# A fused sigmoid attention and SiLU MLP on one core: second matmul started per batch, loads gated in order of use, four score steps around each values group

## The chip, the cores and the metric

The kernel runs on one core of one Trainium2 chip. The metric is the device time of one execution in microseconds (us). Medians of repeated runs are quoted. A verdict of faster or slower needs 2%. "Span" is the profiled time from first to last instruction, some 2 us less than the run's time.

## The reference, cut to what matters

Attention with a sigmoid in place of softmax feeds a two-matrix MLP with SiLU. There are 8 batches, 12 heads, 448 positions and head size 64; the MLP goes from 768 to 2048 and back to 768.

```python
scores = scale * np.matmul(q, k.transpose(0, 1, 3, 2)) - np.log(S)
attn = 1.0 / (1.0 + np.exp(-scores))
x = matmul(attn, v)             # heads merged: (8*448, 768)
h = x @ w_in                    # 768 -> 2048
g = h * (1.0 / (1.0 + np.exp(-h)))
out = g @ w_out                 # 2048 -> 768
```

## The kernel before

The 12 heads of a batch are handled as 3 quads of 4. A quad takes 7 **score steps**: four 64x64 matmuls into one PSUM tile `psc` of two banks, then one sigmoid on ScalarE that writes fp16 attention weights. After 7 steps a **values group** (28 matmuls, `pav`) multiplies them with v. The MLP is a stream of **first-matmul units** (`ph`, 12 matmuls, then a sigmoid on ScalarE and a product on VectorE) and **second-matmul units** (`po`, 32 matmuls, half the columns of 128 output rows). The kernel fixes the order of the instructions on each engine (`manual_schedule`), and the timelines show the work of TensorE (PE) in the Python order below.

```python
ps_sc = tile_pool(name="ps_sc", bufs=2, PSUM)     # two score buffers (4 banks)
ps_1  = tile_pool(name="ps_1",  bufs=4, PSUM)     # everything else   (4 banks)

def scores(b, i, r):
    psc = ps_sc.tile([P, 2, 512], F32, ...)
    for t in range(2):
        for j in range(2):
            nc.tensor.matmul(psc[half(j), t, :S], kT[half(t), r, half(j)], qT[half(t), :, half(j)], ...)
    nc.scalar.activation(attn[b, i][:, :, r, :], psc[:, :, :S], AF.Sigmoid, bias=bias_s, scale=QKSCALE)

# batch 0: attention alone, with dummy matmuls ("idle") between the steps
for i in range(NQ):
    for r in range(R):
        scores(0, i, r)
        ...
        elif r == 3:
            ...
            load_w_in(i)           # quarters 0, 1, 2 of w_in
        if r == 0:
            stage(1, i)            # q and k of batch 1
load_v(1)                          # v of batch 1, behind three quarters of w_in
load_w_in(3)
values(0, NQ - 1)

# batches 1 to 7: two score steps, a values group if one is due, then some GEMM
for n in range(0, len(steps) + VISIT, VISIT):              # VISIT = 2
    for b, i, r in steps[n : n + VISIT]:
        scores(b, i, r)
    if done:
        values(*done.pop())
    ...                                                    # loads, casts, transposes
    if n < len(steps):
        gemm(T_FIRST if steps[n][0] == 1 else T_VISIT)
gemm(1e9)                                                  # the rest of the stream
```

The stream works on pairs of batches: first matmul of batches 0 and 1, then second matmul of both. While batch 1's attention runs, only batch 0's first matmul (16 units) is there to fill PE. v, w_in and w_out are loaded by the GpSimd queue (they are cast on the way), q, k and the transposes by the SyncE queue. One round of the loop, up to its GEMM, is called a **visit** here.

Of the kernel before, what the change touches and what calls it, by code (L numbers as in the profile page):

```python
# [10 lines left out]
F16 = mybir.dt.float16  # L11
F32 = mybir.dt.float32
# [5 lines left out]
def kernel(  # L18
# [13 lines left out]
    nc = tc.nc  # L32

    B, H, S, D = q.shape
    NT, DMODEL = out.shape
    DFF = moe_w_in.shape[1]
    P = 128
# [13 lines left out]
    ps_1 = ctx.enter_context(tc.tile_pool(name="ps_1", bufs=4, space=bass.MemoryType.PSUM))  # L51

    ET = mybir.EngineType
    ctx.enter_context(tc.manual_schedule(engines={ET.PE, ET.Pool, ET.DVE, ET.Activation}))

    qkT = {}
    v16s = {}
# [14 lines left out]

    w_in_sb = cpool.tile([P, NCC, DFF], F16, tag="w_in_sb", name="w_in_sb")
    w_out_sb = cpool.tile([P, NFC, DMODEL], F16, tag="w_out_sb", name="w_out_sb")

    def half(i):
        return slice(i * D, (i + 1) * D)

    def matmul2(ps, lhsT, rhs, start, stop):

        for i in range(2):
            nc.tensor.matmul(ps[half(i)], lhsT[:, half(i)], rhs, start=start, stop=stop)  # L82
# [12 lines left out]
    def load_w_in(step: int):  # L95

        w = DFF // 4
        f = slice(step * w, (step + 1) * w)
        for t in range(2):
            nc.gpsimd.dma_start(  # L100
                w_in_sb[half(t), :, f],
                moe_w_in[t * NCC * D : (t + 1) * NCC * D, f].rearrange("(c d) f -> d c f", d=D),
            )

    def load_w_out(s: int):
        nc.gpsimd.dma_start(
            w_out_sb[:, 4 * s : 4 * s + 4, :],
            moe_w_out[4 * s * P : (4 * s + 4) * P, :].rearrange("(fc p) e -> p fc e", p=P),
        )

    def stage(b: int, i: int, split: bool = False):
        tiles = [
            p2.tile([P, 2, R * D], F32, tag=f"st{nm}", name=f"st{nm}_{b}_{i}", bufs=3)
            for nm in "qk"
        ]
        staged[b, i] = tiles
        for st, src in zip(tiles, (q, k)):
            for t in range(0, 2, 1 if split else 2):
                tn = 1 if split else 2
                pairs_of = src[b].rearrange("(t i j) (p r) d -> i (j p) t (r d)", t=2, j=2, r=R)  # L120
                nc.sync.dma_start(st[:, t : t + tn], pairs_of[i][:, t : t + tn])

    def load_v(b: int, i0: int = 0, i1: int = NQ):
        if i0 == 0:
# [25 lines left out]
    def transpose_dma(b: int, i: int, nm: str):  # L150
        xt = new_T(b, i, nm)
        nc.sync.dma_start_transpose(xt, x16s.pop((nm, b, i)).rearrange("p r t d -> p (r t d)"))
# [14 lines left out]
    def scores(b: int, i: int, r: int):  # L167
        qT, kT = qkT["q", b, i], qkT["k", b, i]
        if r == 0:
            attn[b, i] = p2.tile([P, 2, R, S], F16, tag="attnT", name=f"attnT_{b}_{i}")  # L170
        psc = ps_sc.tile([P, 2, 512], F32, tag="pssc", name=f"psc_{b}_{i}_{r}")
        for t in range(2):
            for j in range(2):
                nc.tensor.matmul(  # L174
                    psc[half(j), t, :S], kT[half(t), r, half(j)], qT[half(t), :, half(j)],
                    start=True, stop=True,
                )
        nc.scalar.activation(  # L178
            attn[b, i][:, :, r, :], psc[:, :, :S], AF.Sigmoid, bias=bias_s, scale=QKSCALE
        )  # L180

# [31 lines left out]
    out_rows = out.rearrange("(b p r) e -> b r p e", b=B, r=R)  # L213

    def h_unit(b, fc):
        m = b // 2
        if m not in gTs:
            gTs[m] = cpool.tile([P, NFC, 2 * S], F16, tag="gTr", name=f"gTr_{m}")
        ph = ps_1.tile([P, 512], F32, tag="ps1", name=f"ph_{b}_{fc}")
        for cc in range(NCC):  # L220
            matmul2(
                ph[:, :S],
                w_in_sb[:, cc, fc * P : (fc + 1) * P],
                xTs[b][:, cc, :],
                cc == 0,
                cc == NCC - 1,
            )
        tsig = p2.tile([P, S], F16, tag="tsig", name=f"tsig_{b}_{fc}", bufs=3)
        nc.scalar.activation(tsig, ph[:, :S], AF.Sigmoid, bias=0.0, scale=ISX)  # L229
        nc.vector.tensor_mul(  # L230
            gTs[m][:, fc, (b % 2) * S : (b % 2) * S + S], ph[:, :S], tsig
        )

    T_H = NCC * 0.187
    T_O = NFC * 0.160 / 2

    def gemm_stream():
        for m in range(B // 2):
            for b in (2 * m, 2 * m + 1):
                while b not in x_done:  # L240
                    yield None
                for fc in range(NFC):
                    h_unit(b, fc)
                    yield T_H
            for g in range(2 * S // P):
                osb = p2.tile([P, DMODEL], F32, tag="osb", name=f"osb_{m}_{g}", bufs=3)
                for nh in range(2):
                    po = ps_1.tile([P, 512], F32, tag="ps1", name=f"po_{m}_{g}_{nh}")
                    for fc in range(NFC):
                        matmul2(  # L250
                            po[:, :NO2],
                            gTs[m][:, fc, g * P : (g + 1) * P],
                            w_out_sb[:, fc, nh * NO2 : (nh + 1) * NO2],
                            fc == 0,
                            fc == NFC - 1,
                        )
                        if fc == NFC // 2 - 1:
                            yield T_O
                    nc.vector.tensor_scalar_mul(
                        osb[:, nh * NO2 : (nh + 1) * NO2], po[:, :NO2], ISX  # L260
                    )
                    yield T_O
                for s in range(2):
                    bl, r = divmod(2 * g + s, R)
                    nc.sync.dma_start(out_rows[2 * m + bl, r], osb[half(s)])

    stream = gemm_stream()
    clock = [0.0, 0.0]

    def gemm(us: float):  # L270
        clock[1] += us
        while clock[0] < clock[1]:
            t = next(stream, None)
            if t is None:
                return
            clock[0] += t
# [16 lines left out]
    for i in range(NQ):  # L293
        nxt = (0, i + 1) if i + 1 < NQ else (1, 0)
        for r in range(R):
            scores(0, i, r)
            if r == 0 and i > 0:
                values(0, i - 1, 0, 4)
            elif r == 1 and i > 0:
                values(0, i - 1, 4, R)  # L300
            elif r == 2:
                transpose_pe(*nxt, "q")
            elif r == 3:
                transpose_pe(*nxt, "k")
                b2, i2 = (nxt[0], nxt[1] + 1) if nxt[1] + 1 < NQ else (1, 0)
                cast(b2, i2, "q", nc.vector)
                cast(b2, i2, "k", nc.gpsimd)
                load_w_in(i)
            else:
                idle(3, f"{i}_{r}")  # L310
            if r == 0:
                stage(1, i)
    load_v(1)
    load_w_in(3)
    values(0, NQ - 1)


    steps = [(b, i, r) for b in range(1, B) for i in range(NQ) for r in range(R)]
    VISIT = 2
    T_FIRST = NFC * T_H / (NQ * R) * VISIT  # L320
    T_VISIT = (NFC * T_H + S / P * NFC * 2 * 0.160) / (NQ * R) * VISIT
    done = []
    for n in range(0, len(steps) + VISIT, VISIT):
        for b, i, r in steps[n : n + VISIT]:
            scores(b, i, r)
        if done:
            values(*done.pop())
        for b, i, r in steps[n : n + VISIT]:
            if r == R - 1:
                done.append((b, i))  # L330
            if r == 0:
                if (b, i) == (1, 2):
                    load_w_out(0)
                    load_w_out(1)
                elif (b, i) == (2, 0):
                    load_w_out(2)
                    load_w_out(3)
                if b + 1 < B:
                    stage(b + 1, i)
                    if i == 0:  # L340
                        load_v(b + 1)
            if r == 3:
                if b == 1 and i + 1 < NQ:
                    for nm in "qk":
                        transpose_pe(1, i + 1, nm)
                    if i + 2 < NQ:
                        cast(1, i + 2, "q", nc.vector)
                        cast(1, i + 2, "k", nc.gpsimd)
                if b + 1 < B:
                    for nm in "qk":  # L350
                        cast(b + 1, i, nm, nc.gpsimd)
                        transpose_dma(b + 1, i, nm)
        if n < len(steps):
            gemm(T_FIRST if steps[n][0] == 1 else T_VISIT)
    gemm(1e9)


# [28 lines left out]
```

## Time and profile before

| | |
|---|---|
| median of runs | 416.78 us (416.7 to 417.35) |
| profiled span | 414.6 us |
| PE busy | 395.6 us, 95% |
| first scores on PE | 8.2 us |
| last matmul ends | 409.7 us |

The first lines are from the page of the kernel before: busy us, share of the span and instructions of PE, then PE's busy tenths, the granted clock and the traffic in 40 slices of 10.4 us.

```profile
PE 395.6 (95%) x5020; PEld 237.8 (57%) x5020; DVE 152.2 (37%) x254; ACT 222.6 (54%) x298; POOL 55.0 (13%) x71
...
PE   7899398999999999999999999999999999999995
...
PEclk9999799999999999999999999999999999999999
...
GB/s 264 306 275 263 185 272 135 190 225 263 185 71 266 298 26 2 125 276 69 77 59 216 294 92 2 98 105 2 77 40 77 40 40 2 2 2 40 78 77 76
```

PE is the limit almost everywhere. One dip stands out: the fifth slice (41 to 52 us) has PE at 3 tenths. Traffic is at 263 to 306 GB/s in the slices before it.

The next lines list what PE waited for in the kernel before: us in total, number of times, longest.

```profile
PE pav_1_0_944 L195 <- DMA v_1_677<-in_v_dram: 6.9, 1, 6.9
...
PE psc_0_1_1291 L174 <- ACT attnT_2_1107 L178: 1.0, 1, 1.0
...
PE psc_0_2_1297 L174 <- ACT attnT_0_1276 L178: 0.5, 1, 0.5
...
PE psc_2_1_1114 L174 <- ACT attnT_1_889 L178: 0.4, 1, 0.4
PE psc_2_5_1232 L174 <- ACT attnT_2_1107 L178: 0.4, 1, 0.4
PE psc_1_0_890 L174 <- ACT attnT_0_713 L178: 0.4, 1, 0.4
```

The largest wait is for v of batch 1; the five others shown are scores that wait for ScalarE to free a score buffer, all in batch 1 or at the start of batch 2. (Left out between them are short waits of the first 25 us, among them 1.2 us for v of batch 0.) The timeline of PE around the largest wait (start us, duration us, engine, line, operation, tiles):

```profile
41.15 0.36 PE L174 MATMUL psc_1_2_938<-qT_1_777,kT_1_794 64*64 64x448 f16 x4
48.44 0.58 PE L195 MATMUL pav_1_0_944<-attnT_0_713,v_1_677 64*64 64x448 f16 x2 [6.93 <-DMA v_1_677<-in_v_dram]
...
48.81 0.58 PE L195 MATMUL pav_1_0_944<-attnT_0_713,v_1_677 64*64 64x448 f16 x2
...
51.20 2.11 PE L82 MATMUL ph_7_977<-xT_401,w_in_sb 128*64 128x448 f16 x12
```

A values pair normally starts every 0.187 us; behind the wait it starts every 0.37 us, and the 12 matmuls of `ph_7` take 2.1 us where 1.3 is usual. The clock has been halved and needs until 53 us to return.

A visit with a values group in the steady part of the kernel before, PE and ScalarE (ACT), lines in between left out:

```profile
148.78 0.38 PE L174 MATMUL psc_2_0_2554<-qT_2_1920,kT_2_1924 64*64 64x448 f16 x4
...
148.99 0.36 PE L174 MATMUL psc_2_1_2560<-qT_2_1920,kT_2_1924 64*64 64x448 f16 x4
...
149.33 1.00 ACT L178 ACTIVATE attnT_2_2553<-psc_2_0_2554,bias_s 128x896 f16<-128x896 f32 x1
...
150.22 1.01 ACT L178 ACTIVATE attnT_2_2553<-psc_2_1_2560,bias_s 128x896 f16<-128x896 f32 x1
150.31 0.35 PE L195 MATMUL pav_3_1_2566<-attnT_1_2277,v_3_1289 64*64 64x448 f16 x2
...
150.60 1.32 PE L82 MATMUL ph_5_2602<-xT_1570,w_in_sb 128*64 128x448 f16 x12
```

Durations of matmuls overlap, so the cost of a unit is read from start to start: a score step 0.19 us, the values group 1.31, a first-matmul unit 1.14, a second-matmul unit 2.60. From one `ph` to the first score costs 0.09 us more than between two `ph`, from the last 64-row matmul back to `ph` 0.10 more (150.31 to 150.60, where 0.19 is usual), and the first units after each change another 0.055: 0.245 us for each **return** from 128-row to 64-row matmuls and back. In this visit PE never waits, but one should note when ScalarE lets go of the second score buffer: 150.22 + 1.01 = 151.23.

### The profile page before, as it was taken

The numbers are of one execution on the slowest core, as the hardware profiler recorded it, in microseconds if no ns is written. First come the engines' busy times: TensorE is split into PE (matmuls) and PEld (weight loads), VectorE is DVE, ScalarE is ACT, GpSimd is POOL, SyncE is SP. The second block draws the span as 40 slices with busy tenths as digits, with TensorE's granted clock in tenths as the row PEclk, the third lists the DMA queues.
The fourth block names the chain that finished last, engine by engine and source line by source line (L and its number), as shares of the span: only waits on it lengthen the run. The fifth ranks groups of instructions, "written<-read, shape, count | busy, mean of one in ns | idle before, by whom it ended". The sixth has DMA issues, their size and how long they took to land.

```text
span 414.6 us, 11185 instructions
## 1 busy us (share of the span) xinstructions
PE 395.6 (95%) x5020; PEld 237.8 (57%) x5020; DVE 152.2 (37%) x254; ACT 222.6 (54%) x298; POOL 55.0 (13%) x71
## 2 busy tenths in 40 slices
PE   7899398999999999999999999999999999999995
PEld 3564154556566555555665555555665655678884
DVE  3545153542221354552221254553222244552221
ACT  3898179675335478676335468666334478340000
POOL 2652050121041000500032000410000000000000
PEclk9999799999999999999999999999999999999999
DMA  8999999999649900991339920850313110001333
GB/s 264 306 275 263 185 272 135 190 225 263 185 71 266 298 26 2 125 276 69 77 59 216 294 92 2 98 105 2 77 40 77 40 40 2 2 2 40 78 77 76
DMA packets 62639, 53.80 MB, mean 130 GB/s; under 512 B 35456, under 2 KB 59008, under 8 KB 62592
## 3 DMA queue, kind: packets, MB, share of 16 engines
q1 hardware_dynamic: 50976, 41.30, 39.2%
q0 software_dynamic: 11616, 11.80, 19.0%
q8 instruction: 39, 0.64, 0.7%
q14 instruction: 8, 0.07, 0.0%
HBM read 45.61 MB, written 11.01 MB: 137 GB/s over the span
## 4 chain that ended last, share of the span: by engine, by line
PE 84%; DMA 10%; ACT 1%; DVE 1%; POOL 1%; issue 1%; SPq 1%; POOLq 0%
DMA v_1_677<-in_v_dram 6%; DMA stk_1_380<-in_k_dram 2%; DMA stk_1_143<-in_k_dram 2%; PE pav_1_0_944 L195 1%; PE po_0_0_4782 L82 1%; PE po_6_0_3863 L82 1%; PE po_2_1_3501 L82 1%; PE po_0_1_3278 L82 1%; PE po_4_1_2188 L82 1%; PE po_6_1_5462 L82 1%; PE po_6_0_5383 L82 1%; PE po_5_1_5346 L82 1%; PE po_4_1_5250 L82 1%; PE po_4_0_5204 L82 1%; PE po_3_1_5167 L82 1%; PE po_2_1_5039 L82 1%
## 5 line engine op out<-in xcount | busy, mean ns | idle before, releaser
L82 PEld LDWEIGHTS <-w_in_sb 128*64 128x64 f16 x1536 | 87.8, 110 | 63.8 <-issue 16.3
L82 PEld LDWEIGHTS <-gTr_5510 128*64 128x64 f16 x448 | 31.4, 110 | 5.1
L82 PEld LDWEIGHTS <-gTr_3998 128*64 128x64 f16 x448 | 24.5, 110 | 13.9 <-issue 3.9
L82 PEld LDWEIGHTS <-gTr_732 128*64 128x64 f16 x448 | 24.4, 110 | 13.9 <-issue 3.9
L82 PEld LDWEIGHTS <-gTr_2460 128*64 128x64 f16 x448 | 24.4, 110 | 13.9 <-issue 3.9
L195 PE MATMUL pav_1_0_944<-attnT_0_713,v_1_677 64*64 64x448 f16 x14 | 2.8, 577 | 6.9 <-DMA v_1_677<-in_v_dram 6.9
L90 PEld LDWEIGHTS <-zeros 64*64 64x64 f16 x180 | 6.2, 121 | 4.4 <-issue 1.7
L195 PEld LDWEIGHTS <-v_1_677 64*64 64x64 f16 x84 | 3.1, 125 | 8.8 <-DMA v_1_677<-in_v_dram 7.4
L229 ACT ACTIVATE tsig_7_990<-ph_7_977 128x448 f16<-128x448 f32 x1 | 0.5, 543 | 10.0 <-PE ph_7_977 L82 10.0
L128 POOL DMA_DIRECT2D v_7_4333<-in_v_dram x1 | 0.8, 818 | 36.6 <-PE pav_5_2_4380 L195 36.6
L128 POOL DMA_DIRECT2D v_5_2795<-in_v_dram x1 | 0.8, 818 | 36.5 <-PE pav_3_2_2842 L195 36.5
L128 POOL DMA_DIRECT2D v_6_3633<-in_v_dram x1 | 0.8, 821 | 35.9 <-PE pav_4_2_3598 L195 35.9
L100 POOL DMA_DIRECT2D w_in_sb<-in_moe_w_in_dram x8 | 5.3, 664 | 0.3 <-DMA w_in_sb<-in_moe_w_in_dram 0.3
L90 PE MATMUL pz_start<-zeros 64*64 64x448 f16 x44 | 4.2, 564 | 1.2 <-DVE bias_s L67 1.2
L178 ACT ACTIVATE attnT_0_197<-psc_0_0_198,bias_s 128x896 f16<-128x896 f32 x1 | 1.0, 1007 | 6.4 <-PE psc_0_0_198 L174 6.4
L195 PEld LDWEIGHTS <-v_0_140 64*64 64x64 f16 x84 | 2.8, 106 | 2.4 <-DMA v_0_140<-in_v_dram 1.5
L208 DVE TENSOR_SCALAR xT_974<-pav_1_0_944 128x448 f16<-128x448 f32 x1 | 0.6, 625 | 9.1 <-PE pav_1_0_945 L195 9.1
L128 POOL DMA_DIRECT2D v_4_2095<-in_v_dram x1 | 0.8, 821 | 23.2 <-PE pav_2_2_2060 L195 23.2
L195 PEld LDWEIGHTS <-v_7_4333 64*64 64x64 f16 x84 | 2.4, 107 | 1.7 <-issue 0.4
L195 PEld LDWEIGHTS <-v_2_730 64*64 64x64 f16 x84 | 2.5, 107 | 1.5
L195 PEld LDWEIGHTS <-v_3_1289 64*64 64x64 f16 x84 | 2.5, 107 | 1.5
L195 PEld LDWEIGHTS <-v_5_2795 64*64 64x64 f16 x84 | 2.5, 107 | 1.5
(1072 smaller groups left out, 955.2 us busy)
## 6 DMA issues: line engine op xcount, KB each, us to landing
w_in_sb<-in_moe_w_in_dram POOLq DMA_DIRECT2D x8, 384.0 KB, 17.7
w_out_sb<-in_moe_w_out_dram POOLq DMA_DIRECT2D x4, 768.0 KB, 19.7
v_0_140<-in_v_dram POOLq DMA_DIRECT2D x3, 224.0 KB, 8.7
v_1_677<-in_v_dram POOLq DMA_DIRECT2D x1, 672.0 KB, 24.8
v_2_730<-in_v_dram POOLq DMA_DIRECT2D x1, 672.0 KB, 30.2
v_3_1289<-in_v_dram POOLq DMA_DIRECT2D x1, 672.0 KB, 16.4
v_4_2095<-in_v_dram POOLq DMA_DIRECT2D x1, 672.0 KB, 6.9
v_5_2795<-in_v_dram POOLq DMA_DIRECT2D x1, 672.0 KB, 6.9
```

Of the source, the lines that this page charges most:

```text
L82: nc.tensor.matmul(ps[half(i)], lhsT[:, half(i)], rhs, start=start, stop=stop)
L90: nc.tensor.matmul(pz[j][half(t), :S], zeros[half(j), :D], zeros[half(j)], start=True, stop=True)
L100: nc.gpsimd.dma_start(w_in_sb[half(t), :, f], moe_w_in[t * NCC * D : (t + 1) * NCC * D, f].rearrange("(c d) f -> d c f", d=D),)
L128: nc.gpsimd.dma_start(v16s[b].rearrange("p t i f -> p (t i) f"), src.rearrange("p t i f -> p (t i) f"))
L178: nc.scalar.activation(attn[b, i][:, :, r, :], psc[:, :, :S], AF.Sigmoid, bias=bias_s, scale=QKSCALE)
L195: nc.tensor.matmul(pav[j][half(t), :S], v16s[b][half(j), t, i, r * D : (r + 1) * D], attnT[half(j), t, r, :], start=(r == 0), stop=(r == R ...
L208: nc.vector.tensor_scalar_mul(xTs[b][:, 2 * i + j, :], pav[j][:, :S], SX)
L229: nc.scalar.activation(tsig, ph[:, :S], AF.Sigmoid, bias=0.0, scale=ISX)
```

## The change

It has four parts: the second matmul of batch b runs right after its first one, instead of per pair of batches, with w_out loaded by column halves so that it can start early; v of batch 1 and the weights are issued in the order of use; loads of q and k are held back by a dependency on the sigmoid of a score step (`behind`), with the SyncE queue in program order; and four score steps stand around each values group, two before and two after, so that PE changes between its two shapes less often. Cut to its core, with some comments added:

```diff
-    def load_w_out(s: int):                       # quarters of the rows
+    def load_w_out(nh: int):                      # halves of the columns
+        e = slice(nh * NO2, (nh + 1) * NO2)
...
+                dma = nc.sync.dma_start(st[:, t : t + tn], pairs_of[i][:, t : t + tn])
+                if behind is not None:
+                    tc.add_manual_dep(dma.ins, behind.ins.name, AFTER, reason="order of loads")
...
-        for m in range(B // 2):
-            for b in (2 * m, 2 * m + 1):
...
+        for b in range(B):
+            while b not in x_done:
+                yield None
+            for fc in range(NFC):
+                h_unit(b, fc)
+                yield T_H
+            order = [(g, nh) for g in tiles_of(b) for nh in range(2)]
+            if b == 0:
+                order.sort(key=lambda u: u[1])    # first half of w_out first
+            for g, nh in order:
+                yield from o_unit(g, nh)
...
                 load_w_in(i)
+                if i == 1:
+                    load_v(1)
-            if r == 0:
-                stage(1, i)
-    load_v(1)
-    load_w_in(3)
+            if (i, r) in ((0, 0), (1, 0), (2, 2)):
+                stage(1, i, behind=act if i else None)
...
+    ends = [(0, 0.0)]                             # how much GEMM is due by which score step
+    for b in range(B - 1):
+        ends.append(((b + 1) * NQ * R + 3, ends[-1][1] + NFC * T_H + len(tiles_of(b)) * 2 * T_O))
...
+            if (i, r) == (0, 2):
+                load_w_in(3)
+            if (i, r) == (1, 0):
+                load_w_out(0)
+            if (i, r) == (1, 4):
+                load_w_out(1)                     # load_v(2) is issued at (1, 1)
...
+                if n == (8 if b == 1 else 0) + 4 * i2:
+                    stage(b + 1, i2, behind=act)
...
+    while n < len(steps) or waiting:
+        now = waiting[:]
+        visit = steps[n : n + (4 if now else 2)]
+        acts = [scores(*s) for s in visit[:2]]
+        for quad in now:
+            values(*quad)
+            waiting.remove(quad)
+        acts += [scores(*s) for s in visit[2:]]
...
+        gemm(stream_at(n) if ... )
```

More of the change, by code (lines that the diff above doesn't have):

```diff
@@ L53 @@
     ET = mybir.EngineType
-    ctx.enter_context(tc.manual_schedule(engines={ET.PE, ET.Pool, ET.DVE, ET.Activation}))
+    ctx.enter_context(tc.manual_schedule(engines={ET.PE, ET.Pool, ET.DVE, ET.Activation, ET.SP}))
     qkT = {}
@@ L74 @@
     w_out_sb = cpool.tile([P, NFC, DMODEL], F16, tag="w_out_sb", name="w_out_sb")
+    AFTER = mybir.DependencyInfo(mybir.DependencyClass.Sync, mybir.DependencyReason.DATA)
     def half(i):
@@ L103, in load_w_in, with stage @@
             )
-    def load_w_out(s: int):
+    def load_w_out(nh: int):
+        e = slice(nh * NO2, (nh + 1) * NO2)
         nc.gpsimd.dma_start(
-            w_out_sb[:, 4 * s : 4 * s + 4, :],
-            moe_w_out[4 * s * P : (4 * s + 4) * P, :].rearrange("(fc p) e -> p fc e", p=P),
+            w_out_sb[:, :, e], moe_w_out[:, e].rearrange("(fc p) e -> p fc e", p=P)
         )
-    def stage(b: int, i: int, split: bool = False):
+    def stage(b: int, i: int, split: bool = False, behind=None):
         tiles = [
@@ L120, in stage @@
                 pairs_of = src[b].rearrange("(t i j) (p r) d -> i (j p) t (r d)", t=2, j=2, r=R)
-                nc.sync.dma_start(st[:, t : t + tn], pairs_of[i][:, t : t + tn])
+                dma = nc.sync.dma_start(st[:, t : t + tn], pairs_of[i][:, t : t + tn])
+                if behind is not None:
+                    tc.add_manual_dep(dma.ins, behind.ins.name, AFTER, reason="order of loads")
     def load_v(b: int, i0: int = 0, i1: int = NQ):
@@ L177, in scores @@
                 )
-        nc.scalar.activation(
+        return nc.scalar.activation(
             attn[b, i][:, :, r, :], psc[:, :, :S], AF.Sigmoid, bias=bias_s, scale=QKSCALE
@@ L215, in h_unit @@
     def h_unit(b, fc):
-        m = b // 2
-        if m not in gTs:
-            gTs[m] = cpool.tile([P, NFC, 2 * S], F16, tag="gTr", name=f"gTr_{m}")
+        if b not in gTs:
+            gTs[b] = p2.tile([P, NFC, S], F16, tag="gT", name=f"gT_{b}")
         ph = ps_1.tile([P, 512], F32, tag="ps1", name=f"ph_{b}_{fc}")
@@ L229, in h_unit, with o_unit @@
         nc.scalar.activation(tsig, ph[:, :S], AF.Sigmoid, bias=0.0, scale=ISX)
-        nc.vector.tensor_mul(
-            gTs[m][:, fc, (b % 2) * S : (b % 2) * S + S], ph[:, :S], tsig
-        )
+        nc.vector.tensor_mul(gTs[b][:, fc, :], ph[:, :S], tsig)
+    osbs = {}
+    def o_unit(g, nh):
+        if g not in osbs:
+            osbs[g] = p2.tile([P, DMODEL], F32, tag="osb", name=f"osb_{g}", bufs=4)
+        osb = osbs[g]
+        blocks = [divmod(2 * g + s, R) for s in range(2)]
+        e = slice(nh * NO2, (nh + 1) * NO2)
+        po = ps_1.tile([P, 512], F32, tag="ps1", name=f"po_{g}_{nh}")
+        for fc in range(NFC):
+            for s, (bl, r) in enumerate(blocks):
+                nc.tensor.matmul(
+                    po[half(s), :NO2],
+                    gTs[bl][:, fc, r * D : (r + 1) * D],
+                    w_out_sb[:, fc, e],
+                    start=(fc == 0),
+                    stop=(fc == NFC - 1),
+                )
+            if fc == NFC // 2 - 1:
+                yield T_O / 2
+        nc.vector.tensor_scalar_mul(osb[:, e], po[:, :NO2], ISX)
+        if nh == 1:
+            for s, (bl, r) in enumerate(blocks):
+                nc.sync.dma_start(out_rows[bl, r], osb[half(s)])
+            del osbs[g]
+        yield T_O / 2
@@ L234, with tiles_of @@
     T_H = NCC * 0.187
-    T_O = NFC * 0.160 / 2
+    T_O = NFC * 0.160
+    def tiles_of(b):
+        return range((R * b) // 2, (R * (b + 1)) // 2)
     def gemm_stream():
-        for m in range(B // 2):
-            for b in (2 * m, 2 * m + 1):
-                while b not in x_done:
-                    yield None
-                for fc in range(NFC):
-                    h_unit(b, fc)
-                    yield T_H
-            for g in range(2 * S // P):
-                osb = p2.tile([P, DMODEL], F32, tag="osb", name=f"osb_{m}_{g}", bufs=3)
-                for nh in range(2):
-                    po = ps_1.tile([P, 512], F32, tag="ps1", name=f"po_{m}_{g}_{nh}")
-                    for fc in range(NFC):
-                        matmul2(
-                            po[:, :NO2],
-                            gTs[m][:, fc, g * P : (g + 1) * P],
-                            w_out_sb[:, fc, nh * NO2 : (nh + 1) * NO2],
-                            fc == 0,
-                            fc == NFC - 1,
-                        )
-                        if fc == NFC // 2 - 1:
-                            yield T_O
-                    nc.vector.tensor_scalar_mul(
-                        osb[:, nh * NO2 : (nh + 1) * NO2], po[:, :NO2], ISX
-                    )
-                    yield T_O
-                for s in range(2):
-                    bl, r = divmod(2 * g + s, R)
-                    nc.sync.dma_start(out_rows[2 * m + bl, r], osb[half(s)])
@@ L267 @@
+        for b in range(B):
+            while b not in x_done:
+                yield None
+            for fc in range(NFC):
+                h_unit(b, fc)
[5 more added lines that the diff above has]
+                yield from o_unit(g, nh)
     stream = gemm_stream()
-    clock = [0.0, 0.0]
-    def gemm(us: float):
-        clock[1] += us
-        while clock[0] < clock[1]:
+    clock = [0.0]
@@ L273, in gemm @@
+    def gemm(until: float):
+        while clock[0] < until:
             t = next(stream, None)
@@ L295 @@
         for r in range(R):
-            scores(0, i, r)
+            act = scores(0, i, r)
             if r == 0 and i > 0:
@@ L308 @@
                 load_w_in(i)
+                if i == 1:
+                    load_v(1)
             else:
                 idle(3, f"{i}_{r}")
-            if r == 0:
-                stage(1, i)
-    load_v(1)
-    load_w_in(3)
+            if (i, r) in ((0, 0), (1, 0), (2, 2)):
+                stage(1, i, behind=act if i else None)
     values(0, NQ - 1)
     steps = [(b, i, r) for b in range(1, B) for i in range(NQ) for r in range(R)]
-    VISIT = 2
-    T_FIRST = NFC * T_H / (NQ * R) * VISIT
@@ L321 @@
-    T_VISIT = (NFC * T_H + S / P * NFC * 2 * 0.160) / (NQ * R) * VISIT
-    done = []
-    for n in range(0, len(steps) + VISIT, VISIT):
-        for b, i, r in steps[n : n + VISIT]:
-            scores(b, i, r)
-        if done:
-            values(*done.pop())
-        for b, i, r in steps[n : n + VISIT]:
-            if r == R - 1:
-                done.append((b, i))
-            if r == 0:
-                if (b, i) == (1, 2):
-                    load_w_out(0)
-                    load_w_out(1)
-                elif (b, i) == (2, 0):
-                    load_w_out(2)
-                    load_w_out(3)
-                if b + 1 < B:
-                    stage(b + 1, i)
-                    if i == 0:
+    ends = [(0, 0.0)]
@@ new lines, with stream_at, side @@
+    for b in range(B - 1):
+        ends.append(((b + 1) * NQ * R + 3, ends[-1][1] + NFC * T_H + len(tiles_of(b)) * 2 * T_O))
+    def stream_at(n):
+        for (n0, t0), (n1, t1) in zip(ends, ends[1:]):
+            if n <= n1:
+                break
+        return t0 + (t1 - t0) * (n - n0) / (n1 - n0)
+    def side(b, i, r, act):
+        if b == 1:
+            if (i, r) == (0, 2):
[4 more added lines that the diff above has]
+                load_w_out(1)
+            if r == 3 and i + 1 < NQ:
+                for nm in "qk":
+                    transpose_pe(1, i + 1, nm)
+            if (i, r) == (1, 0):
+                cast(1, 2, "q", nc.vector)
+                cast(1, 2, "k", nc.gpsimd)
+        if b + 1 < B:
+            n = i * R + r
+            for i2 in range(NQ):
+                if n == (8 if b == 1 else 0) + 4 * i2:
+                    stage(b + 1, i2, behind=act)
+                    if i2 == 0:
@@ L341 @@
                         load_v(b + 1)
-            if r == 3:
-                if b == 1 and i + 1 < NQ:
+                if n == (12 if b == 1 else 6) + 4 * i2:
                     for nm in "qk":
-                        transpose_pe(1, i + 1, nm)
-                    if i + 2 < NQ:
-                        cast(1, i + 2, "q", nc.vector)
-                        cast(1, i + 2, "k", nc.gpsimd)
-                if b + 1 < B:
-                    for nm in "qk":
-                        cast(b + 1, i, nm, nc.gpsimd)
-                        transpose_dma(b + 1, i, nm)
@@ L353 @@
-        if n < len(steps):
-            gemm(T_FIRST if steps[n][0] == 1 else T_VISIT)
+                        cast(b + 1, i2, nm, nc.gpsimd)
+                        transpose_dma(b + 1, i2, nm)
+    waiting = []
+    n = 0
+    while n < len(steps) or waiting:
[6 more added lines that the diff above has]
+        acts += [scores(*s) for s in visit[2:]]
+        for s, act in zip(visit, acts):
+            if s[2] == R - 1:
+                waiting.append(s[:2])
+            side(*s, act)
+        n += len(visit)
+        gemm(stream_at(n) if n < len(steps) else 1e9 if not waiting else stream_at(n - 0.5))
```

## The prediction

> **What bounds it now.** TensorE: the table of engines has PE busy 95% of the 414.6 us span, the chain of waits gives PE 84%. Between 29.3 us (batch 0's attention done) and the last matmul at 409.7 I count in slots from the timeline: score step 0.19, values group 1.31, first-matmul unit 1.14, second-matmul unit 2.60. All units make about 349 us of these 380. The other 31 us:
> - The wait for v of batch 1 (list of waits, PE): 7.1 us from slot to slot, at 41 us. Issued at 23.6, landed at 48.4.
> - Slow clock behind it: values spaced 0.37 instead of 0.187, the next unit 2.04 instead of 1.23: 2.2 us. The Trainium skill ("TensorE: Matmul & The Clock Gate", Part 1) states that the clock halves after about 3.4 us of idleness; this trace agrees.
> - Waits of scores for ScalarE in batch 1, where GEMM pieces of one or two units leave ScalarE behind: five, 3.5 us from slot to slot.
> - 73 to 74 returns from 128-row to 64-row matmuls and back at 0.245 us: 18 us. The skill ("TensorEngine Tiling (Array Packing)", Key Properties) says that changing the tiling mode drains the array; the trace shows that price.
>
> **What the change does.**
> 1. It issues v of batch 1 before the last two quarters of w_in and holds back later q and k. By bytes at about 270 GB/s (slices of the page) v lands near 30 to 36 us and is needed near 44. Wait and slow clock go: -9.3 us.
> 2. Batch 1 gets 29 us of GEMM instead of 18, in pieces of two to five units, so ScalarE no longer trails: -3.5 us. This only moves matmuls out of the final GEMM-only stretch, so moving gains nothing more. The second weight matrix comes early enough (first half needed near 57 us, landed by about 45).
> 3. Grouping: 20 fewer returns by the instruction order: -4.9 us.
> 4. But 20 visits now run score, score, values, score, score with only two score buffers. The fourth step must wait until ScalarE has finished the second. Timeline of before at 148.78: the second sigmoid ends at 151.23, PE would reach the fourth step at 150.69: a stall of 0.59 us after a first-matmul unit; 0.47 after a second-matmul unit (198.42: 200.76 against 200.34). 20 x 0.53 = +10.6 us. So the grouping alone loses about 5.7 us.
> 5. Less traffic at the start: the 1.2 us wait for v of batch 0 may shrink: -0.3 us.
>
> All lies on the critical path, since PE is it. Sum: -9.3 -3.5 -4.9 +10.6 -0.3 = -7.4; 416.8 becomes about 409. I predict **409.0 us**, range **405 to 413**. Chances: faster by over 2% 0.40, within 2% 0.57, slower 0.03.
>
> **What would show each step right or wrong.**
> - PE's waits have no v of batch 1 above 0.5 us; granted clock 1.0 between 40 and 60 us.
> - PE waits for the sigmoid appear about 20 times at some 0.3 us as listed (0.5 from slot to slot), in the fourth score step of a visit with values.
> - GEMM-only end: 16 first-matmul and 8 second-matmul units instead of 16 and 14.
> - From last matmul to span end stays near 4.9 us.
> - Two-step visits keep their 0.245 us.
>
> **What would make it wrong.** If ScalarE frees the score buffer earlier than its record's end, step 4 shrinks and the time nears 403. If gated loads come too late (transposes of batch 2, q and k of batch 1's last group, the second half of w_out behind v of batch 2), new PE waits add several us, possibly with the clock dropping again.

## The result and the profile after

The changed kernel took 411.37 us (409.76 to 411.61, 4 runs) against 416.74 for the kernel before in the same rounds: ratio 0.987, 95% interval 0.983 to 0.990. The gain is clear of noise but under 2%. The predicted 409.0 us was 2.4 us low, within the range.

The page of the changed kernel, the same four lines (slices of 10.2 us):

```profile
PE 391.3 (96%) x5020; PEld 233.3 (57%) x5020; DVE 152.4 (37%) x254; ACT 222.6 (54%) x298; POOL 55.4 (14%) x69
...
PE   8899997999999999999999999999999999999995
...
PEclk9999999999999999999999999999999999999999
...
GB/s 266 255 246 225 224 219 157 198 157 305 150 41 219 156 178 16 152 241 158 27 69 155 221 152 37 78 233 190 92 40 79 40 2 2 40 65 15 2 78 77
```

The dip in the fifth slice has gone. Traffic in the second to fourth slices is lower than before (255, 246 and 225 against 306, 275 and 263 GB/s), not higher.

What PE waited for in the changed kernel, four of its 25 lines:

```profile
PE po_1_1367 L248 <- DMA w_out_sb<-in_moe_w_out_dram: 2.8, 1, 2.8
PE pav_0_0_361 L200 <- DMA v_0_140<-in_v_dram: 1.3, 1, 1.3
...
PE psc_1_4_2574 L179 <- ACT attnT_1_2460 L183: 0.4, 1, 0.4
...
PE psc_2_4_5141 L179 <- ACT attnT_2_5023 L183: 0.3, 1, 0.3
```

No wait for v of batch 1. There are exactly 20 waits of scores for ScalarE, 0.3 to 0.4 us each as listed, one for each visit with a values group and four steps. From slot to slot they lose 0.47 to 0.59 us each and 10.8 us together. At the top stands a wait that was not predicted: for w_out. The predicted place is seen in the timeline of the changed kernel, a visit like the one shown of before (PE and ACT, lines in between left out):

```profile
153.14 0.38 PE L179 MATMUL psc_2_0_2733<-qT_2_1954,kT_2_1958 64*64 64x448 f16 x4
...
153.69 1.00 ACT L183 ACTIVATE attnT_2_2732<-psc_2_0_2733,bias_s 128x896 f16<-128x896 f32 x1
...
154.58 1.01 ACT L183 ACTIVATE attnT_2_2732<-psc_2_1_2739,bias_s 128x896 f16<-128x896 f32 x1
...
154.87 0.36 PE L179 MATMUL psc_2_2_2777<-qT_2_1954,kT_2_1958 64*64 64x448 f16 x4
...
155.64 0.38 PE L179 MATMUL psc_2_3_2783<-qT_2_1954,kT_2_1958 64*64 64x448 f16 x4 [0.42 <-ACT attnT_2_2732 L183]
...
155.96 2.79 PE L248 MATMUL po_0_2798<-w_out_sb,gT_2357 128*64 128x384 f16 x32
```

The third step finds its buffer free: the first sigmoid ended at 154.69. The fourth step would start at 155.06, but the second sigmoid ends at 154.58 + 1.01 = 155.59, and PE starts at 155.64. From the third step to the fourth it is 0.77 us instead of 0.19: 0.58 us lost. In visits that follow second-matmul units it is 0.48 us (172.05 to 172.72): there ScalarE has no first-matmul sigmoid in front of the scores, and its first score sigmoid starts 0.44 us after the scores (170.32 to 170.76) instead of 0.55 (153.14 to 153.69).

The unpredicted wait, in PE's timeline and in the chain of work that ended last (start us, duration us, what):

```profile
65.57 0.36 PE L179 MATMUL psc_2_5_1361<-qT_2_1026,kT_2_1043 64*64 64x448 f16 x4
68.69 2.79 PE L248 MATMUL po_1_1367<-w_out_sb,gT_724 128*64 128x384 f16 x32 [2.77 <-DMA w_out_sb<-in_moe_w_out_dram]
71.42 0.38 PE L179 MATMUL psc_2_6_1403<-qT_2_1026,kT_2_1043 64*64 64x448 f16 x4
```

```profile
37.77 30.89 DMA w_out_sb<-in_moe_w_out_dram
```

The second half of w_out, issued at 37.77, landed 30.9 us later. The fourth second-matmul unit needed it at 65.86 and started at 68.69, so 2.8 us were lost. The first half, issued at 30.90, took 23.0 us by the list of issues: it landed near 54, and was first needed at 54.63.

The end is as predicted: the last matmul to the end of the span took 4.9 us in both kernels. Visits with two steps keep their spacing (340.48, 340.69, 340.98 and 342.14 us for two scores and two `ph`; 144.75, 144.96, 145.25 and 146.41 before). Two smaller forecasts failed: after the last attention work stand 16 first-matmul and 10 second-matmul units, not 16 and 8, and the wait for v of batch 0 did not shrink (1.3 us against 1.2).

### The profile page after: what moved, and what is told of

Its sections match the earlier page's. It is cut to its first block, busy times and chain, and to the rows that moved or that the text cites. A ratio compares the mean times of both kernels' runs of the same rounds, so it can differ in the third digit from the quotient of the medians.

```text
span 409.5 us, 11192 instructions
## 1 busy us (share of the span) xinstructions
PE 391.3 (96%) x5020; PEld 233.3 (57%) x5020; DVE 152.4 (37%) x254; ACT 222.6 (54%) x298; POOL 55.4 (14%) x69
## 4 chain that ended last, share of the span: by engine, by line
PE 73%; DMA 13%; ACT 11%; issue 1%; POOL 0%; SPq 0%; DVE 0%; ACTq 0%; POOLq 0%
DMA w_out_sb<-in_moe_w_out_dram 8%; DMA stk_2_587<-in_k_dram 3%; DMA v_0_140<-in_v_dram 2%; ACT attnT_1_354 L183 1%; DMA stk_0_83<-in_k_dram 1%; ACT attnT_2_518 L183 1%; PE po_1_1367 L248 1%; PE po_0_6030 L248 1%; PE po_0_2971 L248 1%; PE po_0_5909 L248 1%; PE po_0_5838 L248 1%; PE po_0_5359 L248 1%; PE po_0_5219 L248 1%; PE po_0_5148 L248 1%; PE po_1_4604 L248 1%
## 5 line engine op out<-in xcount | busy, mean ns | idle before, releaser
L84 PEld LDWEIGHTS <-w_in_sb 128*64 128x64 f16 x1536 | 84.8, 110 | 61.8 <-issue 8.0
L248 PEld LDWEIGHTS <-gT_724 128*64 128x64 f16 x224 | 14.0, 110 | 10.2 <-DMA w_out_sb<-in_moe_w_out_dram 3.2
L248 PEld LDWEIGHTS <-gT_3896 128*64 128x64 f16 x224 | 14.0, 110 | 7.3 <-issue 1.5
L248 PEld LDWEIGHTS <-gT_2357 128*64 128x64 f16 x224 | 14.0, 110 | 7.3 <-issue 1.5
L248 PEld LDWEIGHTS <-gT_5429 128*64 128x64 f16 x224 | 14.1, 110 | 6.8 <-issue 0.8
L248 PEld LDWEIGHTS <-gT_6100 128*64 128x64 f16 x224 | 14.4, 110 | 4.7
L248 PEld LDWEIGHTS <-gT_3101 128*64 128x64 f16 x224 | 14.1, 110 | 5.2 <-issue 0.8
L248 PEld LDWEIGHTS <-gT_4640 128*64 128x64 f16 x224 | 14.1, 110 | 5.2 <-issue 0.8
L248 PEld LDWEIGHTS <-gT_1562 128*64 128x64 f16 x224 | 14.0, 110 | 5.2 <-issue 0.8
L248 PE MATMUL po_1_1367<-w_out_sb,gT_724 128*64 128x384 f16 x32 | 2.8, 328 | 2.8 <-DMA w_out_sb<-in_moe_w_out_dram 2.8
L183 ACT ACTIVATE attnT_0_197<-psc_0_0_198,bias_s 128x896 f16<-128x896 f32 x1 | 1.0, 1007 | 6.2 <-PE psc_0_0_198 L179 6.2
L133 POOL DMA_DIRECT2D v_6_3823<-in_v_dram x1 | 0.8, 821 | 26.2 <-PE psc_0_2_3807 L179 26.2
L200 PEld LDWEIGHTS <-v_0_140 64*64 64x64 f16 x84 | 2.8, 106 | 2.4 <-DMA v_0_140<-in_v_dram 1.5
L133 POOL DMA_DIRECT2D v_5_2968<-in_v_dram x1 | 0.8, 821 | 24.2 <-PE psc_0_3_3049 L179 24.2
L183 ACT ACTIVATE attnT_2_2732<-psc_2_4_2886,bias_s 128x896 f16<-128x896 f32 x1 | 1.0, 1007 | 5.6 <-PE psc_2_4_2886 L179 5.6
L183 ACT ACTIVATE attnT_2_5023<-psc_2_5_5236,bias_s 128x896 f16<-128x896 f32 x1 | 1.0, 1007 | 5.6 <-PE psc_2_5_5236 L179 5.6
L183 ACT ACTIVATE attnT_2_1945<-psc_2_5_2158,bias_s 128x896 f16<-128x896 f32 x1 | 1.0, 1007 | 5.6 <-PE psc_2_5_2158 L179 5.6
L183 ACT ACTIVATE attnT_2_3484<-psc_2_5_3697,bias_s 128x896 f16<-128x896 f32 x1 | 1.0, 1007 | 5.6 <-PE psc_2_5_3697 L179 5.6
```

What stands on the lines that cost most here:

```text
L84: nc.tensor.matmul(ps[half(i)], lhsT[:, half(i)], rhs, start=start, stop=stop)
L133: nc.gpsimd.dma_start(v16s[b].rearrange("p t i f -> p (t i) f"), src.rearrange("p t i f -> p (t i) f"))
L183: return nc.scalar.activation(attn[b, i][:, :, r, :], psc[:, :, :S], AF.Sigmoid, bias=bias_s, scale=QKSCALE)
L200: nc.tensor.matmul(pav[j][half(t), :S], v16s[b][half(j), t, i, r * D : (r + 1) * D], attnT[half(j), t, r, :], start=(r == 0), stop=(r == R ...
L248: nc.tensor.matmul(po[half(s), :NO2], gTs[bl][:, fc, r * D : (r + 1) * D], w_out_sb[:, fc, e], start=(fc == 0), stop=(fc == NFC - 1),)
```

## The experiments

Two theories stood at the start. **A**: PE is the limit, so times add up: v's wait and slow clock, ScalarE's lag and the returns are saved, the stall of the fourth step and the wait for w_out are paid. **B**: the grouping itself pays, the stall costs nothing that PE would not lose elsewhere, and the rest of the gain was lost in the loads. All runs had five rounds against the kernel before; all results were correct unless it says otherwise. e1 to e4 ran in a first call, in which the kernel before took 416.82 us, e5 to e8 in a second (417.41), e9 to e12 in a third (417.40); the changed kernel itself was measured apart from these and again as e10.

The start of a run varies: the first first-matmul unit begins between 29.2 and 31.7 us in the profiled runs. Where sizes matter, "PE's stretch" is therefore given too: the time from the first first-matmul unit to the end of the last matmul in the profiled run. It is 380.0 us in the kernel before and 375.2 in the changed one.

### e1: two steps in every visit

```diff
-        visit = steps[n : n + (4 if now else 2)]
+        visit = steps[n : n + 2]
```

> The changed kernel with two score steps in every visit, all else kept. Theory A (the stall of the fourth score step costs more than the saved returns): 20 more returns at 0.245 us cost 4.9 us, 20 stalls of about 0.53 us go (10.5 us), so 411.4 becomes about 405.8 us; the list of PE waits has no sigmoid waits in visits with values. Rival B (the grouping pays; PE would lose the stall's time anyway at the next change of mode or to ScalarE): about 416 us. Either way the wait for the second half of w_out (2.8 us) should stay within 1.5 us of what it was.

Measured: 407.04 us, ratio 0.976 (0.973 to 0.978). All waits for the sigmoid in visits with values are gone. Undoing the grouping makes the kernel 4.3 us faster (4.3 in PE's stretch as well), where B expected it 5 us slower. It fell short of A's 405.8, and PE's timeline shows why (matmuls of one kind merged):

```profile
64.61 0.57 PE L179 MATMUL psc<-qT,kT 64*64 64x448 f16 x8
68.39 4.27 PE L248 MATMUL po<-w_out_sb,gT 128*64 128x384 f16 x32 [3.21 <-DMA w_out_sb<-in_moe_w_out_dram]
72.59 0.72 PE L179 MATMUL psc<-qT,kT 64*64 64x448 f16 x8
```

With the grouping gone PE arrived earlier at the second half of w_out and waited 3.3 us (0.5 more), and after this wait the clock was halved: the unit takes 4.2 us from start to start instead of 2.7. So some 2 us of the grouping's cost were hidden by a longer wait for w_out.

### e2: the second half of w_out ahead of v of batch 2

```diff
             if (i, r) == (1, 0):
                 load_w_out(0)
+                load_w_out(1)
-            if (i, r) == (1, 4):
-                load_w_out(1)
```

> The changed kernel with the second half of w_out issued straight after the first, ahead of v of batch 2. Theory A (only the order of the software queue was wrong): the 2.8 us wait goes, v of batch 2 still lands well before its use near 86 us, about 408.6 us. Rival B (the transfers of this stretch as a whole are too slow): the wait moves to the first half of w_out, to q and k of batch 2, or stays; 411 us or more.

Measured: 408.70 us, ratio 0.981 (0.979 to 0.983), as A expected to 0.1 us. The waits for w_out and for v of batch 2 are not on the list; the 20 waits for the sigmoid are:

```profile
PE psc L179 <- ACT attnT L183: 7.4, 20, 0.4
```

### e3: only v of batch 1 earlier, in the kernel before

```diff
                 load_w_in(i)
+                if i == 1:
+                    load_v(1)
...
-    load_v(1)
     load_w_in(3)
```

> The kernel before with one thing changed: v of batch 1 is issued after the second quarter of w_in, not after the third. No gates, no grouping, no early second matmul. Theory A (the order of the software queue alone removes the 7 us wait and the slow clock after it): about 407.5 us, granted clock 1.0 from 40 to 60 us. Rival B (transfers are at their limit there, so without the gates the wait only moves to w_in or v lands little earlier): 412 us or more.

Measured: 413.93 us, ratio 0.994 (0.991 to 0.997). Both theories of this run gave a number, and rival B's is the right one. The profile is of a run that took 415.0 us; the three runs with the highest granted clock (0.998) took 412.6 to 413.7. The waits of PE:

```profile
PE pav L195 <- DMA v<-in_v_dram: 4.1, 2, 3.2
PE psc L174 <- ACT attnT L178: 2.3, 4, 1.0
PE psc L174 <- DMA kT<-xk: 2.0, 1, 2.0
PE ph L82 <- DMA w_in_sb<-in_moe_w_in_dram: 1.5, 2, 0.8
```

v of batch 1 is still waited for (3.2 us of the 4.1; the rest is v of batch 0), the second and third quarters of w_in are now late, and later kT of batch 2 is. This last wait of 2.0 us was followed by a halved clock:

```profile
82.82 0.57 PE L174 MATMUL psc<-qT,kT 64*64 64x448 f16 x8 [1.98 <-DMA kT<-xk]
83.22 2.56 PE L195 MATMUL pav<-attnT,v 64*64 64x448 f16 x28
```

(28 matmuls of values took 2.5 us from start to start instead of 1.4.) So reordering the software queue alone is worth 2.9 us, of the 9.3 that the prediction gave to the order and the gates together.

### e4: only the grouping, in the kernel before

```diff
-    for n in range(0, len(steps) + VISIT, VISIT):
-        for b, i, r in steps[n : n + VISIT]:
+    while n < len(steps) or done:
+        visit = steps[n : n + (4 if done else VISIT)]
+        for b, i, r in visit[:2]:
             scores(b, i, r)
         if done:
             values(*done.pop())
+        for b, i, r in visit[2:]:
+            scores(b, i, r)
...
-            gemm(T_FIRST if steps[n][0] == 1 else T_VISIT)
+            gemm((T_FIRST if steps[n][0] == 1 else T_VISIT) * len(visit) / VISIT)
+        n += len(visit)
```

> The kernel before with four score steps around each values group, nothing else changed. Theory A: 20 fewer returns (-4.9 us) and 19 to 20 stalls of about 0.53 us (+10 us), so 416.7 becomes about 422 us. Rival B (the grouping pays): about 412 us.

Measured: 420.74 us, ratio 1.009 (1.007 to 1.011): the grouping alone makes the kernel 3.9 us slower, not faster. It is less than the 5.3 expected by the medians (PE's stretch is 5.0 us longer):

```profile
PE psc L174 <- ACT attnT L178: 8.5, 21, 1.0
PE pav L195 <- DMA v<-in_v_dram: 8.3, 2, 7.6
```

Of these 21 waits, 18 are new ones of the fourth step and 3 are of the old kind, of which the kernel before had 5. The wait for v of batch 1 grew as well, from 6.9 to 7.6 us.

### e5: both mends, two steps and w_out first

The edits of e1 and e2 together.

> Both mends together: two score steps in every visit, and the second half of w_out ahead of v of batch 2. Theory A (stall of the fourth step, 20 x 0.53 us, against 20 returns, 4.9 us): 5.7 us under the run with only the w_out mend, so about 403.0 us, with no PE wait over 0.5 us after 30 us. If the grouping's net cost is smaller than A says, 404.5 us or more.

Measured: 402.24 us, ratio 0.964 (0.961 to 0.966). The list has no wait of PE after 30 us. Against e2 this is 6.5 us for the grouping by the medians, and 6.1 us in PE's stretch (372.3 to 366.2), somewhat more than the 5.7 of A.

### e6: three steps around a values group

```diff
-        visit = steps[n : n + (4 if now else 2)]
+        visit = steps[n : n + (3 if now else 2)]     # and the edit of e2
```

> As the run with both mends, but three score steps around a values group (two, values, one). The third step needs the first buffer, which ScalarE has freed about 0.1 us before, so no stall; by the instruction order 10 returns fewer than with two steps. Theory A (a return costs 0.245 us of PE's time wherever it is saved without a stall): 2.4 us under the run with two steps, about 400.6 us, no sigmoid waits listed. Rival (saved returns give nothing, PE loses the same elsewhere): 402.5 us or more.

Measured: 400.40 us, ratio 0.959 (0.956 to 0.961); e5 in the same rounds 0.9635. No wait for the sigmoid is listed. The 10 saved returns gave 1.8 us by the medians, 0.18 us each; the two intervals just touch, so this size is not sure. PE's stretch is 366.2 us in e5 and 363.5 in both e6 and e12: 2.7 us, of which 0.2 is a late score in e5 (see e8), so 0.25 us for a return, as read from the timeline before. The timeline of a visit, of this version (e12), with like instructions merged:

```profile
149.28 0.57 PE L179 MATMUL psc<-qT,kT 64*64 64x448 f16 x8
...
149.68 1.49 PE L200 MATMUL pav<-attnT,v 64*64 64x448 f16 x28
149.71 2.80 ACT L183 ACTIVATE attnT<-psc,bias_s 128x896 f16<-128x896 f32 x3 [0.61 <-PE psc L179]
...
151.00 0.36 PE L179 MATMUL psc<-qT,kT 64*64 64x448 f16 x4
```

The step after the values group starts at 151.00, the moment that the group's 28 matmuls allow (149.68 + 1.32). It uses the buffer of the first step, whose sigmoid, 1.0 us long and begun at 149.71, has ended by then.

### e7: without the gates

```diff
-                if behind is not None:
+                if False:                             # and the edit of e2
```

> The changed kernel with the w_out mend, without the gates on loads of q and k (they start when their buffers are free). Theory A (transfers are at their limit from 0 to 45 us, so the gates, not the issue order of v alone, let v of batch 1 land in time): v of batch 1 lands 5 us or more later and PE waits for it or for w_in, 1 to 4 us more than with gates: 410 to 413 us. Rival (issue order alone suffices, gates do nothing): 408.7 us within 0.6.

Measured: 415.58 us, ratio 0.995 (0.993 to 0.997), 6.9 us more than with the gates by the medians (5.9 in PE's stretch). It was worse than A expected, and at another place: v of batch 1 is in time, w_in and the first half of w_out are not:

```profile
PE po L248 <- DMA w_out_sb<-in_moe_w_out_dram: 3.5, 1, 3.5
...
PE ph L84 <- DMA w_in_sb<-in_moe_w_in_dram: 0.5, 1, 0.5
```

The unit behind the 3.5 us wait also ran at a halved clock (4.4 us instead of 2.7). Between 10 and 20 us 301 GB/s were moved, against 255 in e2, but the first half of w_out, issued at 28.8 us, took 30.1 us to land, against 23.3 in e2 (issued at 29.8). So q and k that start as soon as a buffer is free come at the cost of weights that are needed sooner.

### e8: the old spread of the GEMM

```diff
-        ends.append(((b + 1) * NQ * R + 3, ends[-1][1] + NFC * T_H + len(tiles_of(b)) * 2 * T_O))
+        ends.append(((b + 1) * NQ * R, ends[-1][1] + NFC * T_H + (b > 0) * S / P * 2 * T_O))
# and the edits of e1 and e2
```

> As the run with both mends, but with the old spread of the GEMM: batch 1's steps get only batch 0's first matmul. So against the kernel before it has little else than the new loads. Theory A: the waits of scores for ScalarE in batch 1 return (five or so, 3.5 us from slot to slot), about 406.5 us, and 9 to 10 us under the kernel before. Rival (the spread of the GEMM itself is worth more, since it shortens the GEMM-only end): 409 us or more; or it is worth nothing: 403 us.

Measured: 412.27 us, ratio 0.989 (0.986 to 0.992), 10.0 us more than e5. The rival ("worth more") has the number, though not by a shorter end as it had it:

```profile
PE psc L179 <- DMA kT<-xk: 5.5, 1, 5.5
...
PE psc L179 <- ACT attnT L183: 1.1, 3, 0.4
```

With less GEMM in batch 1, PE came to the first score step of batch 2 at about 60 us instead of 68.3 as in e5, and its k was transposed only at 65.8. The unit after the wait ran at a halved clock (4.2 us instead of 2.7). Three waits for ScalarE returned (0.55 us each from slot to slot). From slot to slot these are 5.7, 1.5 and 1.65 us, together 8.9, and PE's stretch is 8.9 us longer than in e5 (375.1 against 366.2), so nothing else of size is left. In e5 too this k has no slack: its transpose was issued at 56.3 us and took 12.1, and a weight load of PE waited 0.3 us for it.

### e9: the old spread, with batch 2's q and k earlier

```diff
-                if n == (8 if b == 1 else 0) + 4 * i2:      # load
+                if n == (4 if b == 1 else 0) + 4 * i2:
-                if n == (12 if b == 1 else 6) + 4 * i2:     # cast and transpose
+                if n == (8 if b == 1 else 6) + 4 * i2:
# and the edits of e8
```

> As the run with the old spread of the GEMM, but q and k of batch 2 are loaded, cast and transposed four score steps earlier, at steps 4 and 8 of batch 1 instead of 8 and 12. Theory A (that run's 5.5 us wait for k of batch 2, with the slow clock after it, came from the old spread reaching batch 2 some 10 us sooner than these loads allow): the wait and the slow clock go (about 7 us), the waits of scores for ScalarE stay: about 405.5 us. Rival B (transfers are at their limit, so the wait moves to another tile): 409 us or more.

The edit moves more than its expectation says: `load_v` stands in the same branch, so v of batch 2 is issued earlier too, at 30.2 us and ahead of w_out (37.0 us and behind it in e8).

Measured: 406.68 us, ratio 0.976 (0.973 to 0.979): 5.6 us of the 10.0 are won back by the medians, less than the 7 of A and more than B allowed. The wait of the profiled run and the unit behind it:

```profile
PE psc L179 <- DMA kT<-xk: 2.6, 1, 2.6
```

```profile
62.59 4.47 PE L248 MATMUL po<-w_out_sb,gT 128*64 128x384 f16 x32
```

The wait shrank by half rather than going. k's transpose was issued at 49.0 us and took 13.2, where the median of this run is 4.2, so the transfers of this stretch limit it. The profiled run is one of the slow ones of its six: it took 408.7 us and another 408.4, at a granted clock of 0.994 and 0.989, and the other four 406.0 to 406.9 at 0.997 or 0.998. The halved clock after the wait (1.7 us in the trace) fits this difference, but the four were not profiled. What ScalarE's lag costs by itself is not isolated by this run: the rest against e5 (4.4 us by the medians) holds this wait, in some runs the halved clock after it, and three waits for ScalarE.

### e10 and e12: the changed kernel and the version with three steps, in the same rounds

> The changed kernel again, unedited, so that it stands in the same rounds as the others: 411.4 us within 0.8.

> The version with three score steps around a values group and the w_out mend again, to stand in the same rounds as the changed kernel: 400.4 us within 0.8, about 2.7% under the changed kernel.

Measured: 410.77 us (ratio 0.985, 0.982 to 0.988) and 400.43 us (0.960, 0.958 to 0.963). The version with three steps and w_out first is 2.5% faster than the changed kernel and 4.0% faster than the kernel before.

### e11: shorter sigmoids where the fourth step waits

```diff
+        W = S // 2 if short else S
+        if short:
+            nc.vector.memset(attn[b, i][:, :, r, W:], 0.0)
-            attn[b, i][:, :, r, :], psc[:, :, :S], AF.Sigmoid, ...
+            attn[b, i][:, :, r, :W], psc[:, :, :W], AF.Sigmoid, ...
...
-        acts = [scores(*s) for s in visit[:2]]
+        acts = [scores(*s, short=bool(now)) for s in visit[:2]]     # and the edit of e2
```

> Wrong result on purpose: the changed kernel with the w_out mend, four score steps kept, PE's order kept, but in visits with values the first two sigmoids work on 224 of 448 columns only (VectorE writes zeros to the rest, 40 small writes). Theory A (the fourth step waits for the end of the second sigmoid): the score buffers come free some 0.8 us earlier, the 20 listed waits go, 408.7 becomes about 398.3 us. Rival B (the time is lost at the change of mode around the larger visit, whatever ScalarE does): 406 us or more.

Measured: 397.60 us, ratio 0.953 (0.950 to 0.955); the result is wrong (relative error 0.34). PE's order and its returns are those of e2, only 40 sigmoids are shorter, and 11.1 us are gone by the medians; no wait for the sigmoid is left on the list. PE's stretch went from 372.3 to 362.2 us, although a new wait for k of batch 2 cost 1.1: 11.3 us without it, and the 20 stalls of e2 lose 10.8 from slot to slot. So the loss is the wait for ScalarE, and not something at the change of shape. The run shortens the first sigmoid as well; that the fourth step waits for the second one is read from the timelines. No run gave the scores a third buffer.

## Why the prediction was right or wrong

- **The total** was right within its range: 409.0 against 411.4. The difference is one term: PE's stretch fell by 4.9 us, and with the 2.8 us of the new wait added back by 7.7, where steps 1 to 4 make 7.1. Step 2 said of the second weight matrix: "first half needed near 57 us, landed by about 45". It was needed at 54.6 and landed near 54, and the second half, which the prediction named only among the things that could go wrong, came 2.8 us late. The prediction shows no working for the 45 us. Its 270 GB/s were too high for this stretch (the slices from the second to the seventh show 255 falling to 157), but that is only part of it: by an estimate from the traffic measured from 30.9 to 54 us (about 5.2 MB), 270 GB/s would have brought the first half near 50. What e2 shows is that the order of the queue was enough to cure the wait: without it the kernel is 2.7 us faster by the medians, 2.1 against e10, whose own wait was 1.8 us.
- **Step 4, the stall of the fourth score step**, was right: 20 waits at the predicted place, 0.47 to 0.59 us each, 10.8 us together where 10.6 was predicted. e11 took 11.1 us away by shortening nothing but sigmoids, where 10.4 was expected. The grouping as a whole costs 4.3 us (e1, with the longer wait for w_out hiding some 2), 6.5 us (e5 against e2; 6.1 in PE's stretch) or 3.9 us (e4, with 18 new stalls; 5.0 in PE's stretch) where 5.7 was predicted.
- **Step 3, the returns**, was right in count (53 in the trace, 73 before) and in price: in e6 ten returns saved without a stall gave 1.8 us by the medians and 2.5 in PE's stretch, where 2.4 was expected.
- **Step 1, v of batch 1**, was right in outcome: no wait, granted clock 1.00 between 40 and 60 us (0.83 before). It was wrong as a cause: "issues v of batch 1 before the last two quarters of w_in and holds back later q and k" was given 9.3 us as if it stood alone, apart from the rest of the change. e3 shows that the issue order alone gives 2.9 us, because v is still 3.2 us late and w_in and kT come late; e7 shows that without the gates the kernel of e2 loses 6 to 7 us. No run has the order and the gates and nothing else, so what the two give together stays open.
- **Step 2, the spread of the GEMM**, was wrong in size and mechanism. "This only moves matmuls out of the final GEMM-only stretch, so moving gains nothing more" overlooked that the moved work also delays the moment at which batch 2's data are needed, from about 60 us (e8) to 68.3 (e5). e8 loses 10.0 us without it, most of it a wait for k of batch 2 with a halved clock after it (7.2 of the 8.9 us in PE's stretch); e9 wins 5.6 back by loading earlier instead. The value of the spread is slack for the transfers, and only then ScalarE's lag: three waits, 1.65 us in e8, where 3.5 were predicted for five. The other two stood at the start of batch 2, where e8 waits for k, so what all five would cost stays open.

The sum came out right because all parts were in place together: wherever the credit belongs, the waits of before went and the stall came. That is in part luck. The prediction named late transposes of batch 2 only as a risk; in e5 their k lands 0.3 us late, and nothing in the prediction saw that the spread is what gives it the time.

## What to carry to other kernels

When PE is the limit, a longer run of one kind of step pays only as far as its output buffers reach: here, with two score buffers, the third step fits behind the values group and the fourth waits for ScalarE, which cost about twice what the saved changes of shape brought (10.8 us against 4.9). Read from the trace when the consumer frees the buffer and when the producer would come back, and choose the group's size by that. While transfers are the limit, moving compute forward or holding loads back can be worth more than the waits it was meant to remove (e8, e7), but such parts don't add up (e3), so test them in pairs.

## What the Trainium skill lacked or had wrong

- "TensorEngine Tiling (Array Packing)", Key Properties, says that changing the tiling mode drains the array, without a price. Here a return from 128-row to 64-row matmuls and back shows 0.245 us in the timeline, and 0.25 us each when ten were saved (e5 against e6 and e12 in PE's stretch; 0.18 by the medians of e5 and e6).
- "TensorE: Matmul & The Clock Gate", Part 1, puts the halving of the clock after an idle window of about 3.4 us, and says that the window runs freely. Here shorter waits did it too: 2.0 us in e3 (values group 2.5 us instead of 1.4) and 2.6 us in the profiled run of e9 (a unit of 4.4 us instead of 2.7), whereas 2.8 us in the changed kernel and 3.2 us in e3's first wait did not. Planning with 3.4 us as a safe limit would be wrong in this kernel. The "this trace agrees" of the prediction rested on one wait of 6.9 us, which cannot tell 3.4 from less.
- "DMA: Bandwidth & Descriptors", Anatomy of one DMA — SWDGE (gpsimd) path, fits one transfer as 2.0 us plus bytes over 436e3. That would make about 5.6 us (an estimate by that fit) for a half of w_out counted as 1536 KB, as it arrives in fp16, and about 9.2 us (an estimate too) for the twice as many bytes read in fp32. Beside other loads, and with its cast, it took 23.0 and 30.9 us here; the page has no figure for transfers of one core that share the engines.
- No page says how a partial group should be sized against the number of PSUM buffers; the number here is one: 0.47 to 0.59 us lost per fourth step with two buffers, none for the third.
